# Dividing three k loads anew over the memory engines, with a table transfer of 96 rows in place of 81

## The chip, the cores and the metric

The kernel runs on one core of one Trainium2 chip. The metric is device time in microseconds for one execution on that core; times are medians over runs of the same program. The core has five compute queues (TensorE, VectorE, ScalarE, GpSimd, and SP, which only issues transfers) and 16 memory engines, which move everything between HBM and the on-chip memory. A transfer issued by GpSimd can change the type on the way; the loads here read float32 from HBM and write 16-bit numbers.

## What is computed

Linear attention on 8 batches, 8 heads, 576 positions and head size 64, followed by a spectral mixing layer over the positions, with 64 complex modes and a 512 x 512 matrix pair for each mode. Cut to what matters:

```python
phi = lambda x: np.where(x > 0, x, np.exp(x) - 1.0) + 1.0
kv  = einsum('bhsd,bhse->bhde', phi(k), v);  z = phi(k).sum(axis=2)
x   = einsum('bhsd,bhde->bhse', phi(q), kv) / (einsum('bhsd,bhd->bhs', phi(q), z)[..., None] + 1e-6)
x   = x.transpose(0, 2, 1, 3).reshape(8, 576, 512)
X   = np.fft.rfft(x, axis=1)[:, :64]
Y   = einsum('bmd,mde->bme', X, w_r + 1j * w_i)
u   = x + np.fft.irfft(Y padded with zeros, n=576, axis=1)
out = u + np.maximum(u @ w_ch, 0.0)
```

The weights `w_r` and `w_i` are 64 x 512 x 512 float32 each, 134 MB together. They are read once and are most of what the kernel moves.

## The kernel before

The kernel has a first stage for the attention and a second one for the modes, and the weights stream in under both.

In the first stage, a loop over the eight batches (`for b in range(B)`) loads q, k and v two batches ahead with `load(b + 2)`, each as one tile of 128 rows of 2304 numbers. The tiles `q16`, `k16` and `v16` have two buffers each, so a load waits until the tile of two batches earlier has been used. ScalarE takes the exponentials (`exps`, L210), VectorE completes the features (`features`, L222 to L234), TensorE turns q, sums `kv` and forms the attention rows (`turn_q`, `sum_kv`, `form_x`), and the rows are transformed with a table of cosines and sines (`transform`, L434). GpSimd issues nearly all loads, in the order in which the program is written (`pin` keeps that order); SP issues the first q load and the table.

The table has 512 + 64 rows of 128 numbers for the positions. Only the first `FROWS = S // 4 - 63 = 81` rows of four of its blocks are loaded, by one transfer at L182 into `fwd_sb[0:81]`; `fold_table` (L336 to L357) makes the other rows from these with small matrix products, by symmetry, and writes rows 64 to 127.

The dictionary `SHARES` names loads that are split by rows into several transfers. A load that isn't named there is one transfer of 128 rows. Before the change it names the k loads of batch 3 (15, 63 and 50 rows) and of batch 5 (5, 77, 35 and 11 rows). The pieces are issued one after the other at L187, and all write the same tile; what uses the tile waits for all of them.

GpSimd also issues the weights: tiles of 128 rows by 16 x 512 numbers, 2 MB on the chip and 4 MB in HBM, each for the real or the imaginary matrices of four modes. `w_ahead` puts the first five between the loads of the batches 3, 5 and 7 (`next(pending)`) and behind them. In the second stage `mode_block` takes one tile after the other: 16 matrix products (L525), then a new tile is issued into the buffer that has come free (`w_get`, `w_load`, L106). The last tile comes in pieces (`w_load_last`, L122), and the products of its pieces, the inverse transform, the channel product and the stores follow it (L960 to L1043).

The memory engines also carry the fetches of the compute queues' own instructions. The page shows them as the queues `q8 instruction` and `q14 instruction`, beside `q0` (what GpSimd issues) and `q1` (what SP issues).

Of the kernel before, what the change touches and what calls it, by code (L numbers as in the profile page):

```python
# [20 lines left out]
def _dft_consts(S: int, NM: int):  # L21

    m = np.arange(NM)
    s_cols = np.concatenate([4 * np.arange(128) + jj for jj in range(4)] + [512 + np.arange(NP)])
    s_rows = np.concatenate([s_cols, s_cols[512:]]).reshape(5, 128).T
    ang = 2.0 * np.pi * s_rows[:, :, None] * m / S
    by_four = np.concatenate([m[g::4] for g in range(4)])
    fwd = np.concatenate([np.cos(ang)[:, :, by_four], -np.sin(ang)[:, :, by_four]], axis=2)

    return fwd.astype(np.float16)  # L30
# [3 lines left out]
def kernel(  # L34
# [10 lines left out]
    nc = tc.nc  # L45
# [6 lines left out]
    NJJ = 4  # L52
# [12 lines left out]

    fwd_np = _dft_consts(S, NM)
    FROWS = S // 4 - 63
    fwd_dr = nc.inline_tensor(np.ascontiguousarray(fwd_np[:FROWS, :4]), name="dft_fwd")

    const = ctx.enter_context(tc.tile_pool(name="const", bufs=1, side="right"))  # L70
    xpool = ctx.enter_context(tc.tile_pool(name="xpool", bufs=1, side="right"))
# [3 lines left out]
    fwd_sb = const.tile([128, 5, 2 * NM], F16, name="fwd_sb")  # L75
# [17 lines left out]
    pin = tc.keep_in_program_order  # L93
# [73 lines left out]

    qT_all = [q_tile(f"qT{b}") for b in range(B)]
    raw, phi, x16s, xfs = {}, {}, {}, {}
    SHARES = {("k", 3): (15, 63, 50), ("k", 5): (5, 77, 35, 11)}  # L170

    def load(b):
        for nm, src in (("q", q), ("k", k), ("v", v)):
            rows_in = src[b].rearrange("h s d -> (h s) d").rearrange(
                "(hp r j) d -> r hp (j d)", r=128, j=2 * NJ
            )
            if (nm, b) == ("q", 0):
                for c in range(2):
                    t = sA.tile([128, 2, NJ * Dh], F32, tag="x16", bufs=2, name=f"q32_{c}")
                    pin(nc.sync.dma_start(out=t, in_=rows_in[:, :, c * NJ * Dh : (c + 1) * NJ * Dh]))  # L180
                    raw[nm, b, c] = t
                pin(nc.sync.dma_start(out=fwd_sb[0:FROWS, 0:NJJ, :], in_=fwd_dr.ap()))  # L182
                continue
            t = sA.tile([128, 2, 2 * NJ * Dh], F16, tag=f"{nm}16", bufs=2, name=f"{nm}16_{b}")
            r0 = 0
            for n in SHARES.get((nm, b), (128,)):
                pin(nc.gpsimd.dma_start(out=t[r0 : r0 + n], in_=rows_in[r0 : r0 + n]))  # L187
                r0 += n
            raw[nm, b] = t
# [259 lines left out]
    def set_diagonal(k: int, of=slice(0, B), copies=(nc.vector.tensor_copy,)):  # L449
        for g in range(4):  # L450
            rows = slice(32 * g, 32 * g + 32)
            src = xt[rows, of, :, k : XK : NQ - 1].rearrange("p b c t -> p c t b")
            pin(copies[g % len(copies)](out=xz[k % 2][rows, :, :, g, of], in_=src))  # L453

    load(0)
    load(1)
    ones_where(id16, -1, 1, 0)
    make_turns()
# [4 lines left out]
    for b in range(B):  # L463
        if b + 2 < B:
            load(b + 2)
            if b % 2 == 1:
                next(pending)
            if b == 2:
                pin(nc.gpsimd.memset(xz[0], 0.0))
        turn_q(b, 0)  # L470
        turn_q(b, 1)
        if b == 0:
            fold_table()
        sum_kv(b)
        if b + 1 < B:
            for _ in features(b + 1):
                pass
        if b + 2 < B:
            exps(b + 2)
        for jj in range(NJJ + 1):  # L480
            form_x(b, jj)
            if b == 0 and jj == 0:
                make_place()
            if b > 1 and jj == 1:
                place_x(b - 2)
            if b > 0 and jj in (2, 3):
                transform(b - 1, jj - 2)
        if b > 0:
            transform(b - 1, 2)
            transform(b - 1, 3)  # L490
# [245 lines left out]
    def x_of(t: int):  # L736
        if t < B * NJJ:
            return x_main[t // NJJ][:, t % NJJ, :]
        i = t - B * NJJ
        return x_tail[i // 2][:, i % 2, :]  # L740
# [234 lines left out]
    for b in range(B):  # L975
        pairs += [(b * NJJ, b * NJJ + 1), (b * NJJ + 2, b * NJJ + 3)]
        if b % 4 == 3:
            k = b // 4
# [251 lines left out]
    for i, t in enumerate(pairs[0]):  # L1230
# [4 lines left out]
                out=x_of(t), in0=accs[0][:, i], scalar=0.0, in1=x_of(t), op0=ALU.max, op1=ALU.add  # L1235
# [60 lines left out]
```

## Time and profile before

| | |
|---|---|
| median of 3 runs | 417.84 us (417.62 to 417.85) |
| the profiled run | 417.94 us, of which the span of the page is 416.2 us |
| PE busy | 304.5 us, 73% of the span |
| VectorE busy | 243.7 us, 59% |
| ScalarE busy | 148.5 us, 36% |
| GpSimd busy | 51.9 us, 12% |
| moved by the memory engines | 92.84 MB as written, 163.66 MB read from HBM |
| time to landing, k loads | 7.9 us at least, 11.3 median, 15.2 at most |

The page counts an engine as busy when it executes; issuing a transfer isn't counted, except on GpSimd. The line for DMA gives, in 40 equal slices of the span, the mean busy share of the 16 memory engines in tenths. The chain is the work that ended last, followed back from the last instruction to whatever released each step. The trace under the page holds more: for every transfer the times of its 16 landing marks (each memory engine adds one to the transfer's semaphore when its part has landed), and for every packet its start, duration, size and queue, though not the engine that moved it.

### The profile page before, as it was taken

To read this page: it belongs to the slowest core of one execution; us is meant where nothing else is said; L and a number is where in the kernel's file an instruction comes from. 1 tells how busy PE (TensorE), PEld (TensorE's weight loads), DVE (VectorE), ACT (ScalarE), POOL (GpSimd) and SP (SyncE) were. 2 spreads that over 40 slices of the span, in tenths; PEclk is the share of its full clock that TensorE was granted. 3 is DMA by queue.
4 is the path that set the end of the run, shared out by engine and by line. 5 is a ranking of instruction groups with operands and counts; after the bars stand their busy time and mean duration, and the time that the engine had idled before them with its cause. 6 is when DMAs were issued, how large, how long until landed. Compare 5 with 4: busy or idle time off the path is not lost.

```text
span 416.2 us, 6713 instructions
## 1 busy us (share of the span) xinstructions
PE 304.5 (73%) x2767; PEld 171.4 (41%) x2767; DVE 243.7 (59%) x542; ACT 148.5 (36%) x220; POOL 51.9 (12%) x91
## 2 busy tenths in 40 slices
PE   0269799999583466576665466988978887887993
PEld 0167677777341233233332233443433333452431
DVE  3779978995732654557474442555455644722795
ACT  4667787864300001000000112244443442322583
POOL 6233423100110000000000000000100000230200
PEclk9999955788688558666666679789999999999997
DMA  8999999999999999999999999999999999999698
GB/s 216 211 211 217 208 221 202 226 217 213 217 213 216 217 219 219 211 218 219 216 219 211 219 217 217 219 212 217 218 216 222 209 219 217 213 212 195 216 402 344
DMA packets 16652, 92.84 MB, mean 223 GB/s; under 512 B 2054, under 2 KB 2807, under 8 KB 12335
## 3 DMA queue, kind: packets, MB, share of 16 engines
q0 software_dynamic: 12816, 81.70, 94.3%
q1 hardware_dynamic: 3806, 10.73, 6.8%
q8 instruction: 21, 0.34, 0.3%
q14 instruction: 9, 0.07, 0.0%
HBM read 163.66 MB, written 9.44 MB: 416 GB/s over the span
## 4 chain that ended last, share of the span: by engine, by line
DMA 53%; PE 26%; DVE 12%; ACT 3%; issue 3%; POOL 2%; DVEq 0%; ACTq 0%; POOLq 0%
DMA w<-in_moe_w_r_dram 33%; DMA w<-in_moe_w_i_dram 16%; PE P L525 9%; PE kvp L264 5%; DVE x_main L1043 3%; DMA k<-in_k_dram 3%; DVE x L300 3%; PE qTp L244 3%; PE eps L906 2%; PE xf L434 2%; DVE xz L453 1%; PE num L158 1%; ACT qT L251 1%; ACT ke L210 1%; DVE rd L297 1%
## 5 line engine op out<-in xcount | busy, mean ns | idle before, releaser
L525 PE MATMUL P<-w,xz 128*64 128x512 bf16 x480 | 82.9, 507 | 51.6 <-DMA w<-in_moe_w_r_dram 24.6
L525 PEld LDWEIGHTS <-xz 128*64 128x64 bf16 x480 | 39.1, 138 | 84.8 <-issue 72.6
L536 ACT CAST ys<-P 128x512 f16<-128x512 f32 x8 | 4.7, 585 | 115.6 <-PE P L525 115.6
L906 PE MATMUL eps<-wch,xTw 128*128 128x512 f16 x144 | 37.5, 385 | 3.8 <-DVE xTw L898 3.8
L887 DVE TENSOR_TENSOR x_main<-ya,x_main 128x512 f32<-128x512 f32 x32 | 21.9, 688 | 28.5 <-PE ya L883 28.2
L889 ACT CAST x16w<-x_main 128x512 f16<-128x512 f32 x32 | 19.8, 618 | 44.2 <-DVE x_main L887 43.3
L453 DVE COPY xz<-xt 32x384 bf16<-32x384 bf16 (+2 forms) x62 | 31.4, 507 | 2.1 <-ACT xt L419 1.2
L264 PE MATMUL kvp<-vpad,ke 32*128 32x130 f16 x576 | 23.4, 265 | 8.3 <-ACT qT L251 8.3
L837 PE MATMUL nw<-kv_diag,qT 128*128 128x130 f16 (+1 forms) x160 | 21.7, 261 | 10.3 <-DVE x_main L850 4.4
L914 ACT CAST E<-eps 128x512 f16<-128x512 f32 (+1 forms) x40 | 21.1, 539 | 22.1 <-PE eps L906 22.1
L534 DVE CAST ys<-P 128x512 f16<-128x512 f32 x10 | 6.9, 691 | 33.3 <-PE P L525 33.3
L264 PEld LDWEIGHTS <-ke 32*128 32x128 f16 x576 | 21.8, 117 | 9.7 <-issue 9.4
L244 PE MATMUL qTp<-id,qe 128*128 128x128 f16 x144 | 16.8, 310 | 11.3 <-DVE qe L228 9.6
L106 POOL DMA_DIRECT2D w<-in_moe_w_i_dram x15 | 8.0, 532 | 136.0 <-PE P L525 82.5
L106 POOL DMA_DIRECT2D w<-in_moe_w_r_dram x16 | 8.7, 545 | 124.5 <-PE P L525 114.9
L300 DVE TENSOR_TENSOR x<-num,rd 128x512 f16<-128x512 f32 x32 | 22.1, 691 | 1.1
L837 PEld LDWEIGHTS <-qT 128*128 128x128 f16 (+1 forms) x160 | 13.3, 125 | 22.6 <-issue 13.2
L898 DVE COPY xTw<-xTp 128x512 f16<-128x512 f16 x36 | 14.9, 416 | 9.8 <-PE xTp L896 9.7
L158 PE MATMUL num<-kv_sb,qT 64*128 64x65 f16 (+1 forms) x320 | 16.1, 220 | 6.1 <-DVE x L300 3.9
L251 ACT COPY qT<-qTp 128x1152 f16<-128x1152 f16 x16 | 19.5, 1282 | 2.6 <-PE qTp L244 2.0
L244 PEld LDWEIGHTS <-qe 128*128 128x128 f16 x144 | 14.6, 146 | 12.4 <-DVE qe L228 10.0
L848 DVE RECIPROCAL rdw<-nw 128x4 f32<-128x4 f32 (+1 forms) x40 | 7.0, 176 | 20.8 <-PE nw L837 20.4
(162 smaller groups left out, 501.0 us busy)
## 6 DMA issues: line engine op xcount, KB each, us to landing
w<-in_moe_w_i_dram POOLq DMA_DIRECT2D x15, 2048.0 KB, 17.0
w<-in_moe_w_r_dram POOLq DMA_DIRECT2D x14, 2048.0 KB, 15.5
out_dram<-x_main SPq DMA_DIRECT2D x14, 512.0 KB, 3.2
v<-in_v_dram POOLq DMA_DIRECT2D x8, 576.0 KB, 14.0
q<-in_q_dram POOLq DMA_DIRECT2D x7, 576.0 KB, 12.7
k<-in_k_dram POOLq DMA_DIRECT2D x6, 576.0 KB, 12.6
w<-in_moe_w_r_dram POOLq DMA_DIRECT2D x2, 1024.0 KB, 16.6
w<-in_moe_w_r_dram POOLq DMA_DIRECT2D x4, 512.0 KB, 11.9
```

The costliest lines, as they stand in the source:

```text
L158: mm = nc.tensor.matmul(num[hpo][orow, c0 : c0 + 65], qT[rows, hpp, h2, cols], kv_sb[rows, hpp, h2, :])
L244: nc.tensor.transpose(qT_ps[:, j], phi["q", b][:, c, j].rearrange("p o d -> p (o d)"), id16,)
L251: nc.scalar.copy(out=qT[:, :, c * NJ : (c + 1) * NJ], in_=qT_ps.rearrange("p j x -> p x j"))
L264: nc.tensor.matmul(kv_ps[:, h2, 0:130], phi["k", b][r0 : r0 + 32, j // NJ, j % NJ].rearrange("p o d -> p (o d)"), vp[r0 : r0 + 32, :, j, 0 ...
L300: nc.vector.tensor_tensor(out=dst.rearrange("p (o c d) -> p o c d", o=2, c=4), in0=nv[:, :, :, 0:64], in1=rden.unsqueeze(3).broadcast_to([ ...
L453: pin(copies[g % len(copies)](out=xz[k % 2][rows, :, :, g, of], in_=src))
L525: nc.tensor.matmul(P[c : c + width, :], x, w[:, dc, :], start=first, stop=last, tile_position=(0, c), skip_group_check=True,)
L837: nc.tensor.matmul(num[c][orow, h2 * 130 : h2 * 130 + 130], qT[:, c, h2, rows_of(jj, BASE[b % 2])], kv_diag[:, b, c, h2].rearrange("p o n ...
L887: pin(nc.vector.tensor_tensor(out=x, in0=acc, in1=x, op=ALU.add))
L889: pin(nc.scalar.copy(out=x16w[t], in_=x))
L906: nc.tensor.matmul(e_ps, xT[:, c, :], wch16[:, c, :], start=(c == 0), stop=(c == NDC - 1))
L914: pin(nc.scalar.copy(out=dst, in_=e_ps[:, cols]))
```

## The change

The diff has three parts. The k load of batch 3 is split into 15, 100 and 13 rows in place of 15, 63 and 50. The k load of batch 4, one transfer before, is split into 6, 22, 98 and 2 rows. That of batch 5 is split into 54, 25, 39 and 10 rows in place of 5, 77, 35 and 11. And the table's transfer takes 96 rows, the next multiple of 16 above 81; the additional rows 81 to 95 are true rows of the table, and `fold_table` still reads the first 81 and overwrites rows 64 to 127.

```diff
     FROWS = S // 4 - 63
-    fwd_dr = nc.inline_tensor(np.ascontiguousarray(fwd_np[:FROWS, :4]), name="dft_fwd")
+    LROWS = -(-FROWS // 16) * 16
+    fwd_dr = nc.inline_tensor(np.ascontiguousarray(fwd_np[:LROWS, :4]), name="dft_fwd")
...
-    SHARES = {("k", 3): (15, 63, 50), ("k", 5): (5, 77, 35, 11)}
+    SHARES = {("k", 3): (15, 100, 13), ("k", 4): (6, 22, 98, 2), ("k", 5): (54, 25, 39, 10)}
...
-                pin(nc.sync.dma_start(out=fwd_sb[0:FROWS, 0:NJJ, :], in_=fwd_dr.ap()))
+                pin(nc.sync.dma_start(out=fwd_sb[0:LROWS, 0:NJJ, :], in_=fwd_dr.ap()))
```

No byte of q, k, v or the weights is added or left out; the table grows from 81 KB to 96 KB.

## The prediction

> **What bounds the kernel now.** I read the chain of waits first, by engine and then in order of time, because the change touches nothing but transfers.
>
> ```profile
> DMA 53%; PE 26%; DVE 12%; ACT 3%; issue 3%; POOL 2%; DVEq 0%; ACTq 0%; POOLq 0%
> ```
>
> ```profile
> 349.37 17.05 DMA w<-in_moe_w_i_dram
> 366.46 1.93 PE P L525 x16
> 368.69 2.73 POOL w L122 x5
> 371.60 13.84 DMA w<-in_moe_w_i_dram
> 388.65 1.08 PE acc L960 x5
> ```
>
> From 119.58 us on, the chain is nearly all weight transfers, with TensorE between them, and behind the last one it is a fixed tail (the last piece lands at 386.11, the span ends at 416.2). So the question is when the last weight piece lands. The table of DMA queues says what fills the time:
>
> ```profile
> DMA  8999999999999999999999999999999999999698
> q0 software_dynamic: 12816, 81.70, 94.3%
> q1 hardware_dynamic: 3806, 10.73, 6.8%
> q8 instruction: 21, 0.34, 0.3%
> q14 instruction: 9, 0.07, 0.0%
> ```
>
> The 16 memory engines are busy from the first loads to the last weights, and a transfer has landed only when the slowest of its engines has. The trace keeps, for each transfer, 16 landing marks, one an engine. For the last weight piece they are 383.12, 383.61, 384.18, 384.41, 384.50, 384.51, 384.57, 384.89, 384.94, 385.31, 385.67, 385.74, 385.81, 385.82, 385.93 and 386.11: a spread of 2.99 us, mean 384.95. Evening them out could gain 1.16 us at most; whoever gets more work on one of the late engines loses directly. The change is a new division of rows over engines, so I work out each engine's own account.
>
> **Who carries which rows now.** In the packet records, the packets of one engine follow each other at exactly 173 ns for q, k and v (two to a row, so 0.346 us a row), the same on all 16, so engines can be followed by their phase. For the split k load of batch 3, runs of 14 packets (7 rows) appear on nine engines for the 63 rows, and of 10 packets (5 rows) on ten engines for the 50; the 15 rows go to fifteen. In batch 5, 77 rows go to eleven engines and 35 to seven. The count is the largest number up to 16 that divides the rows, and each split transfer begins at the engine after the last of the one before; no other order fits the marks. I call the engine with the first row 0. The table's 81 rows lie on engines 0 to 8, nine each: after it seven engines land the first k load at 8.58 to 8.76 and nine at 9.09 to 9.24, about 0.46 us apart, 0.051 us a row.
>
> Two other things load an engine: the instruction fetches in q8 and q14. A 16 KB fetch of q8 delays one engine's stream by 1.12 us; 20 of them come before the end, and they go round eight engines: 9 to 14 and two of 4, 5, 6. Of q14, five fetches (at 38.0, 96.0, 183.8, 278.8 and 358.0, where VectorE has executed some 110 to 140 more recorded instructions each time) cost 0.53 us each and all fall on one engine of the pair 2, 3; two of 0.32 fall on one of 0, 1.
>
> **The change, engine by engine.** By the same division, the rows of k loads 3, 4 and 5 together (24 would be even) and the last landing become:
>
> | engines | rows before | rows after | table | landing before | landing after |
> |---|---|---|---|---|---|
> | 0, 1 | 29 | 29 | -0.15 | 385.31, 385.74 | 385.16, 385.59 |
> | 2, 3 | 23 | 27 | -0.15 | 383.61, 385.81 | 384.84, 387.04 |
> | 4 | 22 | 27 | -0.15 | 383.12 | 384.70 |
> | 5, 6 | 22 | 19 | -0.15 | 384.94, 386.11 | 383.75, 384.92 |
> | 7 | 28 | 29 | -0.15 | 384.89 | 385.09 |
> | 8 | 26 | 29 | -0.15 | 384.18 | 385.07 |
> | 9 to 14 | 22 | 20 | +0.31 | 384.50 to 385.93 | 384.12 to 385.55 |
> | 15 | 28 | 29 | +0.31 | 384.41 | 385.07 |
>
> The rows of engine 2, for instance: of batch 3 one of the 15, ten of the 100 and one of the 13; of batch 4 none, two of the 22, seven of the 98, none; of batch 5 none, five of the 25, none, one of the 10: 27. The table column is 96 rows on all sixteen, six each, against nine or none: minus 3 or plus 6 rows of 0.051 us. Engine 2 or 3 then: 385.81 + 4 x 0.346 - 0.15 = 387.04.
>
> The choice in it is which of 4, 5, 6 is which, for they had the same rows before. One of the three took no q8 fetch and is the earliest of all; I take it for 4, so that the fetching engines are neighbours (5, 6). Were 4 the middle one, it would land at 384.94 + 1.58 = 386.52 and change nothing at the top.
>
> Common to all: batch 4 becomes four transfers instead of one, three more closing marks of 0.022 us, and each split transfer brings some 32 extra packets of four bytes (224 now with seven, at 6 to 22 ns); four more make eight an engine, 0.05 to 0.1 us. I take 0.1 for both together, between nothing and 0.2. The last landing goes from 386.11 to 387.14, **1.03 us later**. The profiled run took 417.94 (span 416.2 and 1.7 around it), so 418.97 against it; it lies 0.1 above the median of 417.84, which gives **418.9**.
>
> What else the edit does is covered. GpSimd issues three more transfers:
>
> ```profile
> 35.95 0.72 POOL L187 DMA_DIRECT2D k<-in_k_dram  x1 [1.42 <-issue]
> 36.81 0.71 POOL L187 DMA_DIRECT2D v<-in_v_dram  x1
> 37.52 1.40 POOL L469 MEMSET xz<- 128x1536 bf16 x1
> 43.86 0.72 POOL L187 DMA_DIRECT2D q<-in_q_dram  x1 [4.94 <-ACT qT L251]
> 46.09 2.52 POOL L187 DMA_DIRECT2D k<-in_k_dram  x4 [1.51 <-ACT kv_sb L276]
> ```
>
> Four pieces cost 2.52 where one costs 0.72, so 1.8 us. Behind it stand the v load, the memset of xz and the q load; the q load has 4.94 us of idle time before it, and the v load's data cannot move before the k load's has (46.3 to 49.3). Without that cover it is 1.8 us. On SP the table is still one issue. ScalarE's exponentials of k start at 38.36, 49.37 and 60.35 for batches 3 to 5, and the slowest pieces land at 36.11, 49.27 and 58.32; batch 3 stays near 36.3, and batch 4 may come some tenths late on engines that now carry nine rows. That stretch is followed by weights already in the queue until 121, so a delay of some tenths there reaches the end as nothing; without cover, as itself.
>
> The Trainium skill, "DMA: Bandwidth & Descriptors", section "Why a DMA increments its semaphore by 16 and not by 1", has the same largest-divisor rule, but also an exception in which GpSimd's direct copies use all engines with the row count divided by 16 and rounded up, 100 rows on engines 0 to 14. By that exception engines 0 to 9 would carry some 28 to 30 rows and the end would come about 2 us later, near 420. The trace here speaks against it: 63 rows went to nine engines, seven each, not to sixteen.
>
> **The rivals.** First, engine 4 is the heavy one of its three: it lands at 386.11 + 1.58 + 0.1 = 387.79, 1.68 later, 419.5. For it: rows alone cannot tell; against it: two neighbours would then have unlike loads.
>
> Second, on the other side: VectorE's five fetches sit on another engine in the changed program. Then the engine that is last is one of 0, 1 or of 9 to 14, at 385.59 + 0.1 = 385.69, which is 0.42 earlier: 417.4. It decides as soon as fewer than three of the five remain there (387.14 less 2 x 0.53 is under 386.11). For it: I know one execution of one program; and without this engine the new accounts are strikingly even (383.75 to 385.6). Against it: all five fell on one engine, at intervals that only VectorE's instruction count explains, and that count does not change.
>
> Third, the spread is hidden: something other than the slowest engine ends the chain, and the time stays 417.8. Against it: TensorE waits for weights at every step of the chain, and the piece that lands last is the one that ends it.
>
> Fourth, one of the two mishaps above: rounded-up division (420), or the GpSimd delay uncovered (419.6).
>
> **How the numbers follow.** The forecast has 0.62, engine 4 heavy 0.12, the fetches elsewhere 0.15, no effect 0.06, the fourth 0.05. A measurement of this kernel can tell about 0.2%, 0.84 us, from no change; 1.03 is not far above it, so of the forecast I count 0.08 as within it. Slower: 0.54 + 0.12 + 0.05 = 0.71. Faster by over 0.84 would need nearly the whole 1.16 us of unevenness gone: 0.03. The rest, 0.26, is within. The forecast's own range, from the 0 to 0.2 of extra packets and 0.2 of scatter between runs and marks, is 418.5 to 419.3; the whole range reaches to the fetches elsewhere and to the heavy engine 4: 417.3 to 419.7.
>
> **What would show it.** In the changed kernel: the 16 marks of the first k load lie together (no two groups 0.46 apart); runs of 20 packets on ten engines in batch 3 and of 14 on fourteen in batch 4; four k issues of about 2.5 us at 36 us on GpSimd; the last weight piece lands near 387.1, with one engine more than a microsecond behind the other fifteen, the one that took VectorE's fetches. If the marks of the last piece lie within 2 us of each other and end before 386, the second rival was right and I am wrong; if they end at 387 and the span does not move, the third.

## The result, and the profile after

The changed kernel takes 419.03 us (median of 9 runs, 418.88 to 419.06) against 417.84 before (9 runs, 417.62 to 418.22): 1.0027 times as long, 95% interval 1.0018 to 1.0036. It is slower by 1.19 us (0.8 to 1.5 by the interval). The profiled run took 419.05, of which the span is 417.2.

The shares of the chain of waits by engine, and the tables of DMA use and queues, of the changed kernel:

```profile
DMA  8999999999999999999999999999999999999698
...
q0 software_dynamic: 12960, 81.70, 94.2%
q1 hardware_dynamic: 3828, 10.75, 6.8%
q8 instruction: 21, 0.34, 0.3%
q14 instruction: 8, 0.07, 0.0%
...
DMA 56%; PE 24%; DVE 10%; ACT 3%; issue 3%; POOL 2%; ACTq 0%; DVEq 0%; POOLq 0%
```

As many bytes as before go through queue q0, at the same mean use. It has 144 packets more (12960 against 12816), all of four bytes, which the split transfers bring. Nothing in these averages says that the kernel got slower. Only the chain has three points more of DMA; three points are 12 us, another way of the chain through the first stage (its share of k loads goes from 3% to 6%), and not the microsecond that was lost. In order of time (start, duration, what), the end of the chain:

```profile
349.87 17.58 DMA w<-in_moe_w_i_dram
...
367.49 1.93 PE P L526 x16
...
369.71 2.16 POOL w L123 x4
371.86 13.94 DMA w<-in_moe_w_i_dram
```

Up to the product these are the steps of before, 1.03 us later (the product started at 366.46). Then the chain goes through another piece of the last tile than before: of the pieces that GpSimd issues from there on it is the fifth, before it was the sixth, so these two lines are not to be compared. The fifth piece was issued at 370.84 and landed at 384.80 before; it is issued at 371.86 and lands at 385.81 now, 1.01 later. The last piece has its last landing mark at 387.13, before at 386.11: 1.02 us later. The span grew by 1.0, so all of the difference is there when the last weights land, and nothing is added behind them.

Where it came from is seen earlier. Two stretches of the chain, of the changed kernel and then of the kernel before:

```profile
263.80 16.45 DMA w<-in_moe_w_r_dram
...
280.29 3.62 PE P L526 x16
...
300.77 1.87 PE P L526 x16
...
302.92 15.54 DMA w<-in_moe_w_r_dram
```

```profile
263.16 15.42 DMA w<-in_moe_w_r_dram
...
278.62 3.60 PE P L525 x16
...
298.11 1.87 PE P L525 x16
...
300.26 17.75 DMA w<-in_moe_w_r_dram
```

The product that waits for the tile issued at 263 starts 1.67 us later than before, and the product at 300 is 2.66 later. The landing marks of single tiles show why. Ordinary lines from the trace's landing records; issue time, then the 16 marks in order:

```
before 263.16: 276.28 276.77 277.21 277.36 277.49 277.64 277.70 277.73 277.76 277.93 277.94 277.99 278.03 278.06 278.44 278.58
after  263.80: 276.43 277.09 277.34 277.42 277.47 277.55 277.56 277.71 277.76 277.99 278.07 278.33 278.34 278.40 278.56 280.25
after  284.21: 296.46 296.74 296.75 296.80 296.87 296.88 297.09 297.11 297.32 297.46 297.75 297.76 297.79 297.81 297.95 299.13
after  294.75: 306.77 306.84 306.85 306.95 307.01 307.11 307.13 307.36 307.39 307.40 307.46 307.47 307.48 307.94 308.34 308.78
last piece   : 384.61 384.64 384.79 384.83 384.92 384.97 385.24 385.25 385.26 385.27 385.75 385.97 386.10 386.27 386.43 387.13
```

At 280.25 one engine is 1.69 us behind the next, while the other fifteen are about where they were before. Followed by its phase in the packet records, this engine takes one of VectorE's fetches at 278.9, just before its last packet of this tile, and it is the one that takes those at 182.7 and 359.3 too. It makes the products shown wait, and a product that starts later frees its weight buffer later. So the tile issued at 292.09 before is issued at 294.75. The early engines have then nothing left: their last packets of the previous tile end from 296.1 to 297.1, and the first packets of the new one start from 296.35 on and take up to 1.83 us in place of 1.23. The engines lose 3.9 us together there (1.6 in gaps, 2.3 in longer packets), about half a microsecond for each of eight.

The delays of the issues do not add up to the end: the tile that is issued 2.66 us later lands only 0.47 later (308.78; before, 308.31), since the late engine still had packets queued. The lead of the fifteen over the one, 1.18 at the tile before, is 0.44 there, mainly because one of the fifteen took a fetch of TensorE's at 303.2 in between. At the end the lead is 0.70. The last step, from 0.45 us behind the kernel before (357.20 against 356.75 for the tile issued at 340.11, before at 339.62) to 1.03 (367.45 against 366.42 for the next), comes with VectorE's fetch at 359.3 (before, 358.0), which falls on the engine that is last now; in the kernel before it fell on one that was not.

What the edit does to GpSimd's queue is covered. GpSimd's timeline of the changed kernel (start, duration, instruction, and in brackets the idle time before it and what ended that):

```profile
36.01 2.46 POOL L188 DMA_DIRECT2D k<-in_k_dram  x4 [1.51 <-ACT kv_sb L277]
38.46 0.76 POOL L188 DMA_DIRECT2D v<-in_v_dram  x1
39.20 1.42 POOL L470 MEMSET xz<- 128x1536 bf16 x1
43.81 0.73 POOL L188 DMA_DIRECT2D q<-in_q_dram  x1 [3.20 <-DMA w<-in_moe_w_r_dram]
```

The v load is issued 1.65 us later than before, and the idle time in front of the q load falls from 4.94 to 3.20; the q load itself starts at 43.81 against 43.86.

### The profile page after: what moved, and what is told of

The parts are those of the page before. It is cut to its first block, busy times and chain, and to the rows that moved or that the text cites. A ratio compares the mean times of both kernels' runs of the same rounds, so it can differ in the third digit from the quotient of the medians.

```text
span 417.2 us, 6718 instructions
## 1 busy us (share of the span) xinstructions
PE 305.6 (73%) x2767; PEld 171.6 (41%) x2767; DVE 243.6 (58%) x542; ACT 148.5 (36%) x220; POOL 55.2 (13%) x94
## 3 DMA queue, kind: packets, MB, share of 16 engines
q0 software_dynamic: 12960, 81.70, 94.2%
## 4 chain that ended last, share of the span: by engine, by line
DMA 56%; PE 24%; DVE 10%; ACT 3%; issue 3%; POOL 2%; ACTq 0%; DVEq 0%; POOLq 0%
DMA w<-in_moe_w_r_dram 32%; DMA w<-in_moe_w_i_dram 18%; PE P L526 9%; DMA k<-in_k_dram 6%; DVE x_main L1044 3%; PE kvp L265 3%; DVE x L301 2%; PE eps L907 2%; PE xf L435 2%; PE qTp L245 2%; PE num L159 1%; ACT qT L252 1%; PE xf L440 1%; DVE xz L454 1%; PE acc L961 1%
## 5 line engine op out<-in xcount | busy, mean ns | idle before, releaser
L454 DVE COPY xz<-xt 32x384 bf16<-32x384 bf16 (+2 forms) x62 | 31.4, 507 | 2.1 <-ACT xt L420 1.2
L907 PEld LDWEIGHTS <-xTw 128*128 128x128 f16 x144 | 12.6, 100 | 15.8 <-DVE xTw L899 4.4
```

Source lines behind the costliest of these rows:

```text
L907: nc.tensor.matmul(e_ps, xT[:, c, :], wch16[:, c, :], start=(c == 0), stop=(c == NDC - 1))
```

## The experiments

Eleven kernels, each timed beside the kernel before on the same chip (its median there was 417.88 to 418.05). All change `SHARES` or the table of the kernel before, or both, and nothing else; diffs are against the kernel before. "Rows" are those of the k loads 3, 4 and 5 on one engine together, with 24 if they were even.

**The two parts apart.** The table alone, with the old shares:

```diff
+    LROWS = -(-FROWS // 16) * 16
-    fwd_dr = nc.inline_tensor(np.ascontiguousarray(fwd_np[:FROWS, :4]), name="dft_fwd")
+    fwd_dr = nc.inline_tensor(np.ascontiguousarray(fwd_np[:LROWS, :4]), name="dft_fwd")
-                pin(nc.sync.dma_start(out=fwd_sb[0:FROWS, 0:NJJ, :], in_=fwd_dr.ap()))
+                pin(nc.sync.dma_start(out=fwd_sb[0:LROWS, 0:NJJ, :], in_=fwd_dr.ap()))
```

> The table's 96 rows alone, with the old shares. Theory of the engine accounts: engines 0 to 8 lose three table rows (0.15 us), 9 to 15 gain six (0.31); the latest of 9 to 14 goes from 385.93 to 386.24 and becomes the last, 0.13 later than before: 418.0 us, no change that can be told. Rival, that the table is what costs the time: 419.0.

418.17 us against 418.05, ratio 1.0003 (0.9994 to 1.0012); the last mark is at 386.30. No difference that the measurement can tell.

The shares alone, with the old table:

```diff
-    SHARES = {("k", 3): (15, 63, 50), ("k", 5): (5, 77, 35, 11)}
+    SHARES = {("k", 3): (15, 100, 13), ("k", 4): (6, 22, 98, 2), ("k", 5): (54, 25, 39, 10)}
```

> The new shares alone, with the table of 81 rows. Engine accounts: the engine of the pair 2, 3 that takes VectorE's fetches gains four rows and keeps its nine table rows, so it lands the last piece at 387.13 + 0.15 = 387.28, alone at the end, 1.17 later than before: 419.0 to 419.1 us. Rival, that the table is what costs the time: 417.8.

419.10 against 418.05, 1.0027 (1.0017 to 1.0037); the last mark is at 387.22, and the one before it at 386.03: the others lead by 1.19, where the changed kernel has 0.70. The packet records show no pause of the early engines near 296 here. The shares are the whole loss, and it does not need that pause.

**More transfers and more issues, with even rows.** Batch 4 in four equal pieces of 32 rows, two on each engine, so that each engine keeps its rows:

```diff
-    SHARES = {("k", 3): (15, 63, 50), ("k", 5): (5, 77, 35, 11)}
+    SHARES = {("k", 3): (15, 63, 50), ("k", 4): (32, 32, 32, 32), ("k", 5): (5, 77, 35, 11)}
```

> The kernel before with the k load of batch 4 in four transfers of 32 rows, which lie two rows to an engine on all sixteen: GpSimd issues as many transfers for batch 4 as in the changed kernel, and no engine carries other rows. Engine accounts: three more closing marks of 0.022 us, 386.17, 417.9 us, the same as before. Rival, that the additional issues on GpSimd (1.8 us of its time) are what costs the microsecond: 419.0.

418.26 against 418.05, 1.0006 (0.9997 to 1.0014), last mark 386.32. The issues stand on GpSimd as in the changed kernel:

```profile
36.10 2.20 POOL L187 DMA_DIRECT2D k<-in_k_dram  x4 [1.46 <-ACT kv_sb L276]
38.28 0.74 POOL L187 DMA_DIRECT2D v<-in_v_dram  x1
```

So neither the later issues nor the three transfers more cost a microsecond. By this one execution the three cost up to 0.21 together.

**Even rows, first attempt.** A division meant to relieve the late engines, with two pieces of a single row:

```diff
-    SHARES = {("k", 3): (15, 63, 50), ("k", 5): (5, 77, 35, 11)}
+    SHARES = {("k", 3): (14, 1, 100, 13), ("k", 4): (1, 63, 25, 39), ("k", 5): (25, 88, 15)}
```

> Old table; k loads of batch 3 in 14, 1, 100, 13 rows, of batch 4 in 1, 63, 25, 39, of batch 5 in 25, 88, 15. It has as many transfers as the changed kernel (11), but engines 2 and 3 carry 23 rows as in the kernel before, 5, 6 and 9 to 14 carry 21, and 0, 1, 7, 8, 15 carry 28 to 30. Engine accounts: the late engines all come out between 385.4 and 385.8, plus 0.1 for the additional transfers: last mark near 385.9, 417.6 us, 0.2 faster than before and 1.4 faster than the changed kernel. Rival, that splitting into more transfers is itself what costs the time: 419.0.

A miss: 420.91 against 418.05, 1.0076 (1.0062 to 1.0089), with marks from 385.75 to 388.22. My account gave a single row to one engine. If a row of one is passed over and the next dimension of the tile, which is 2, is divided, the piece goes to two engines, and every later transfer begins one engine further on for each such piece. Then engine 3 has 28 rows and engine 9 has 30, and the last landing comes out between 387.4 and 388.8, which holds the 388.22. The error was in my account of single rows; no kernel after this one has any.

**Which engine is the late one.** The 23 rows of the engines 2 and 3 were equal before and their 27 are equal after, so neither kernel tells them apart. Two divisions that load one of them and not the other:

```diff
-    SHARES = {("k", 3): (15, 63, 50), ("k", 5): (5, 77, 35, 11)}
+    SHARES = {("k", 3): (54, 11, 63), ("k", 4): (49, 75, 4), ("k", 5): (22, 5, 98, 3)}
```

> Old table; batch 3 in 54, 11, 63 rows, batch 4 in 49, 75, 4, batch 5 in 22, 5, 98, 3: engine 2 carries 27 rows, engine 3 23, all others about what they carry in the kernel before (28 on 0 and 1, 21 on 5 and 6, 22 on 9 to 14). It and the next kernel tell which of the two takes VectorE's fetches. Engine accounts: if it is engine 2, the last piece lands at 387.25, alone at the end, 1.1 us after the kernel before; if it is engine 3, engine 2 lands at 385.05 and the last is one of 9 to 14 at 386.0, the same as before. Exactly one of the two kernels is slower. Rival, that the divisions cost by their number or by their spread over all engines: both alike, 10 and 11 transfers.

417.66 against 417.97, 0.9995 (0.9986 to 1.0003); last mark 385.75, although the engines 2 and 4 carry 27 rows. From the chain of waits:

```profile
368.33 2.73 POOL w L122 x5
371.27 13.84 DMA w<-in_moe_w_i_dram
```

```diff
-    SHARES = {("k", 3): (15, 63, 50), ("k", 5): (5, 77, 35, 11)}
+    SHARES = {("k", 3): (25, 18, 20, 65), ("k", 4): (28, 90, 5, 5), ("k", 5): (11, 54, 63)}
```

> Old table; batch 3 in 25, 18, 20, 65 rows, batch 4 in 28, 90, 5, 5, batch 5 in 11, 54, 63: engine 3 carries 27 rows, engine 2 23, the others about as in the kernel before. Engine accounts: slower by 1.1 us (last mark 387.27) if engine 3 takes VectorE's fetches, the same as before (386.0) if engine 2 does. Rival, number or spread of the transfers: as the kernel with 27 rows on engine 2.

419.38 against 417.97, 1.0035 (1.0023 to 1.0047); last mark 387.28, the one before it 386.02. The chain's end:

```profile
369.86 2.16 POOL w L122 x4
372.02 13.99 DMA w<-in_moe_w_i_dram
```

The two chains go through different pieces of the last tile, the sixth and the fifth of those issued there. The fifth was issued at 370.49 and landed at 384.46 with 27 rows on engine 2; with 27 on engine 3 it is issued 1.53 us later and takes as long. The other fifteen lead by 1.26 there. Exactly one of the two kernels is slower: the late engine is engine 3, and engine 4 with 27 rows, in both, isn't.

**More on the same engine.** Both engines with 31 rows:

```diff
-    SHARES = {("k", 3): (15, 63, 50), ("k", 5): (5, 77, 35, 11)}
+    SHARES = {("k", 3): (7, 77, 35, 9), ("k", 4): (77, 49, 2), ("k", 5): (9, 54, 65)}
```

> Old table; batch 3 in 7, 77, 35, 9 rows, batch 4 in 77, 49, 2, batch 5 in 9, 54, 65: engines 2 and 3 carry 31 rows, eight more than in the kernel before and four more than in the changed one; no other engine carries more than before but 4. Engine accounts: the cost goes up by 0.346 us a row; the last mark at 385.81 + 8 x 0.346 + 0.06 = 388.64, 2.5 us after the kernel before, so about 420.3 to 420.5 us. Rival, that the end moves with the spread of all engines and not with this one: about 419, as the changed kernel.

420.70 against 417.97, 1.0072 (1.0057 to 1.0086); last mark 388.89. The chain's end:

```profile
371.47 2.15 POOL w L122 x4
373.62 13.95 DMA w<-in_moe_w_i_dram
```

With 23, 27 and 31 rows, all with the old table, engine 3 lands at 385.81, at 387.22 to 387.28, and at 388.89: 1.4 to 1.5 us for the first four rows and 1.6 to 1.7 for the next four, where four rows alone are 1.38. The 0.2 to 0.3 above that in the second step lie mainly in two tiles: the last marks of the tiles issued at 148.44 and 158.12 come 9.86 and 9.87 us after those of the tile before, where three27 has 9.68 and 9.71. Why was not followed up. The other fifteen end between 385.75 and 387.33 here, later than with three27 (383.82 to 386.02), as engines that wait for the one.

**Which engines get TensorE's fetches how often.** Of the 20 fetches before the end, eight engines get two or three each. If the round always began at the same engine, some of the engines 9 to 14 would always have three, and could be relieved. Two divisions, one with fewer rows on 9, 10 and 11 (20) and the other with fewer on 12, 13 and 14 (20):

```diff
-    SHARES = {("k", 3): (15, 63, 50), ("k", 5): (5, 77, 35, 11)}
+    SHARES = {("k", 3): (40, 54, 21, 13), ("k", 4): (65, 25, 3, 35), ("k", 5): (4, 84, 15, 25)}
```

> Old table; batch 3 in 40, 54, 21, 13 rows, batch 4 in 65, 25, 3, 35, batch 5 in 4, 84, 15, 25. Engine 3, which the last runs showed to take VectorE's fetches, carries 21, its neighbour 2 carries 28; 0 and 1 carry 28; 5, 6, 9, 10 and 11 carry 20; 12 to 14 carry 24. The open question is the order in which TensorE's fetches go round: 20 of them on eight engines, so some of 9 to 14 have three and some two. If 9, 10, 11 have three (order 6, 9, 10 and so on upward): all late engines come out between 385.1 and 385.4, last mark near 385.5, 0.5 to 0.6 us faster than the kernel before and 1.7 faster than the changed one. If 12, 13, 14 have three: 385.93 + 2 x 0.346 = 386.6, 0.5 to 0.6 slower than before. Rival, that the number of transfers (12) sets the time: slower than the changed kernel.

418.89 against 417.96, 1.0019 (1.001 to 1.0027).

```diff
-    SHARES = {("k", 3): (15, 63, 50), ("k", 5): (5, 77, 35, 11)}
+    SHARES = {("k", 3): (15, 81, 32), ("k", 4): (99, 4, 25), ("k", 5): (11, 63, 54)}
```

> Old table; batch 3 in 15, 81, 32 rows, batch 4 in 99, 4, 25, batch 5 in 11, 63, 54: as the kernel above, but 9, 10 and 11 carry 24 rows and 12 to 14 carry 20. If 9, 10, 11 have three of TensorE's fetches: last mark 386.6 to 386.7, 0.6 us slower than before. If 12, 13, 14 have: 385.5, 0.5 us faster. Exactly one of the two should be faster than the kernel before; a mixed order would leave both near 386.6.

418.62 against 417.96, 1.0012 (1.0002 to 1.0021). One of the two should have been faster; both are slower, so a round with a fixed beginning that runs upward is out. The single runs show more. Of the eleven runs of each kernel, in us:

```
light912    417.93 417.98 | 418.75 418.76 418.79 418.89 418.96 419.00 419.03 419.17 419.17
light1214   417.43        | 418.40 418.40 418.42 418.53 418.62 418.62 418.63 418.63 418.65 418.66
```

They fall into two times some 0.8 to 1.2 us apart, which is about one fetch (1.12). The profiled run of light1214 has three marks late, 386.51, 386.69 and 386.69, the next at 385.72: three engines of 24 rows with three fetches, for which the account gives 386.6. That the round begins at different engines in different runs fits both, but no run here follows the beginning, so it stays open.

**The change without its heavy engine.** The old table, and shares that leave the engines 0 to 2, 7, 8 and 15 with 29 or 30 rows, about as the change has them (engine 2: 27), but give the engines 3 and 4 21 rows in place of 27:

```diff
-    SHARES = {("k", 3): (15, 63, 50), ("k", 5): (5, 77, 35, 11)}
+    SHARES = {("k", 3): (7, 108, 4, 9), ("k", 4): (15, 100, 13), ("k", 5): (33, 21, 52, 22)}
```

> Old table; batch 3 in 7, 108, 4, 9 rows, batch 4 in 15, 100, 13, batch 5 in 33, 21, 52, 22: 11 transfers and nearly the division of the changed kernel (29 or 30 rows on 0, 1, 7, 8, 15; 21 on 6 and 9 to 14, 19 on 5), but engine 3 carries 21 rows in place of 27. Engine accounts: with all of TensorE's fetching engines equal, it no longer matters which of them has three fetches; the late ones come out at 385.6 to 385.75, the last mark near 385.8, 0.3 us faster than the kernel before and 1.3 faster than the changed one, in all runs alike. Rival, that a division this uneven or this many transfers cost by themselves: 418.9.

417.76 (417.51 to 417.87) against 417.88, 0.9994 (0.9985 to 1.0003). The marks of the last piece lie between 384.27 and 385.80, with no engine apart. The chain's end:

```profile
368.38 2.16 POOL w L122 x4
370.54 13.94 DMA w<-in_moe_w_i_dram
```

That piece is issued 1.32 us earlier than in the changed kernel and takes as long. With as many k transfers of these three batches as the changed kernel has (eleven; eight before), this is 1.27 us less than the changed kernel's median. That it would be 0.3 us faster than the kernel before isn't shown: 0.12 was measured, within the noise.

The same thought with fewer pieces, batch 5 whole, and with the three lines of the table of 96 rows as in t96:

```diff
-    SHARES = {("k", 3): (15, 63, 50), ("k", 5): (5, 77, 35, 11)}
+    SHARES = {("k", 3): (7, 108, 13), ("k", 4): (15, 100, 13)}
```

> The table of 96 rows; batch 3 in 7, 108, 13 rows, batch 4 in 15, 100, 13, batch 5 whole: six transfers, 30 rows on 0, 1 and 2, 22 on 3, 20 on 9 to 14. Engine accounts: the last mark at 385.74 + 0.346 - 0.15 = 385.94 on one of 0, 1, so 0.1 to 0.2 us faster than the kernel before, which cannot be told from it: 417.7. If it is faster than the kernel with 11 transfers, the transfers cost more than the 0.02 us each that I gave them.

417.91 against 417.88, 0.9999 (0.999 to 1.0008); last mark 385.80. Of all divisions, two27 and relieved have the lowest medians, 0.1 to 0.3 us under the kernel before, and with intervals that reach 1.0003 neither can be told from it.

## Why the prediction was right, and where it wasn't

- **The end is set by the last landing of the slowest engine:** right. The last mark moved by 1.02 us and the span by 1.0. The rival that the spread is hidden fell with the dose of 23, 27 and 31 rows.
- **The heavy engine and its landing:** right. 387.14 was worked out, 387.13 measured. That the two agree to 0.01 is luck: by s81 the additional transfers cost 0.03 where 0.1 was put, the table saves 0.09 where 0.15 was put, and the two errors cancel. The rows alone, 1.38, carry the result. The engine is 3, shown by two27 and three27; the account could only say 2 or 3, and the number was the same for both.
- **Which of 4, 5 and 6 is which:** the choice held. Engine 4 with 27 rows isn't late (two27), so the rival with 419.5 fell.
- **VectorE's fetches stay where they are:** right. In the trace after, five of them come at 37.7, 96.1, 182.7, 278.9 and 359.3, where VectorE has executed within one instruction as many as before. The rival on the other side needed them elsewhere; its condition is off by one, since 387.14 less 2 x 0.53 leaves three of the five in place, not fewer than three. What it would have looked like is shown by relieved: no engine apart, a last mark of 385.80 (385.69 was worked out), and 417.76.
- **The table:** right in size and in kind. The marks of the first k load lie in one group, 8.74 to 9.20, where two groups stood before; on engine 3 it saves 0.09 (387.22 without, 387.13 with), 0.15 was worked out.
- **The additional transfers, 0.1 in a range of 0 to 0.2:** the size stays open in that range. Engine 3 alone (s81, 387.22 against 387.04 + 0.15 worked out without them) makes it 0.03 for three, k4x4 0.21, each from a single execution. The extra packets of four bytes are 144, nine an engine, where eight were worked out.
- **The cover on GpSimd:** right. The four issues take 2.46 us, the q load behind them starts on time, and k4x4 has the same issues without the loss.
- **The division by largest divisors:** right for the pieces of more than one row. Followed by their phase, four runs of exactly 20 packets begin at 31.4 to 31.5 us and ten of exactly 14 between 42.9 and 48.3; the others join neighbouring loads in the records and can't be counted (ten and fourteen were worked out), so the end is the better witness: for rounded-up division some 420 was worked out. Level showed what my account of it lacked, single rows.
- **"One engine more than a microsecond behind the other fifteen":** wrong; it was 0.70. The step that failed is the table of landings for the other engines, worked out as if each ran without a pause. The latest of them was worked out at 385.69, with the 0.1 for the transfers; it ended at 386.43. In this run the engines that are ahead ran out of work once, near 296, and lost 3.9 us together; the late engine did not, which is why its own number was untouched. How much of the 0.74 that pause makes isn't shown, since the records don't name the engines and cannot follow one across it. The sign itself was not a bad one: with the same rows and the old table (s81) the lead is 1.19, with 27 rows on engine 3 and others elsewhere (three27) it is 1.26, and neither has such a pause there.
- **The time:** 418.97 was worked out for a profiled run and 418.9 for the median; measured were 419.05 and 419.03. The 0.1 taken off for the profiled run's place above the median did not come back: the profiled run after is 0.02 above its median.

## What to carry to other kernels

Where transfers fill a kernel, mean use and bytes say little: keep an account for each memory engine of rows and of instruction fetches, and look for the one that ends last. A row moved from one engine to another is paid in full on the engine that is latest and gains nothing on one that is early, since the last landing alone is waited for. Before dividing loads "evenly", find which engine has work that isn't in the program: here equal rows were not equal work, and 4 rows of 1.38 us put on the wrong engine were the whole loss.

## What the runs showed of the hardware

- The five fetches of VectorE's instructions that delay a stream by 0.53 us each fall on the same memory engine, 3, in the kernels that were made to tell it from engine 2 (417.66 with 27 rows on engine 2, 419.38 with 27 on engine 3).
- How often each of the eight engines gets one of TensorE's fetches seems not to be the same from run to run; kernels with unlike rows on these engines (light912, light1214) show two times about 1 us apart. Of the kernels with like rows most show one; three27 and both31 have one run each well above the others (420.17 against 419.27 to 419.43, and 422.56 against 420.60 to 420.81), which isn't explained.
- The excess of one late engine shows in full as time (1.02 us). How far it lies behind the next engine says less: 0.70 in the changed kernel, where early engines once ran dry, 1.19 in s81 and 1.26 in three27.
- A transfer of one row behaves as if divided over its next dimension, 2: worked out from the time of one kernel (level), not shown by packets.
